# Small filter operations moved from VectorE to GpSimd, a product half split by output block, and a new order in a fused mixer kernel

## The chip, the cores and the metric

The kernel runs on one core of a Trainium2 chip. The metric is device time in microseconds of one execution, as the median of several runs. A core has five engines that run their own queues in order and wait for each other by semaphores: TensorE (PE, matrix products into PSUM), VectorE (DVE), ScalarE (ACT), GpSimd (POOL) and SyncE (SP, which here only issues DMAs). DMAs are also issued from the queues of ScalarE and GpSimd.

## The reference

The inputs are in bfloat16, with S = 2048 positions, D = 640 channels and F = 1536. Two branches of the same input are mixed by a gate of one value a position:

```python
x = A_q
g = sigmoid((x * gate_w).sum(-1, keepdims=True))
# A: a shift convolution of four taps on k, times v, then a causal convolution over the whole length
kv = sum(shifted(k, t) * shift_k[:, ks - 1 - t] for t in range(4)) * v
y  = irfft(rfft(pad(kv)) * rfft(pad(ssm_k)))[:S] + kv * ssm_D      # per channel, length 2S
a  = q * y
# B: an MLP mixer, whose channel quarters are shifted by +1, -1, +2, -2 positions
h  = gelu(layernorm(x) @ w1)
x1 = x + shifted_quarters(h) @ w2
b  = x1 + gelu(layernorm(x1) @ w3) @ w4
out = g * a + (1 - g) * b
```

## The kernel before

**How it is written.** The program first records some 1170 operations, each with its engine, its inputs and its outputs, and derives from the overlaps of their memory which must wait for which. A table `SEQUENCE` then gives the order in which all operations are emitted; each engine gets its own in that order, and runs them in that order. A table `PLACES` gives each PSUM tile its bank, and a tile that takes over a bank waits for the users of the one before. A string `ON` of zeros and ones turns single choices round: each call of `turn(default)` takes the next digit and decides between two engines for one operation (or between an engine and a DMA queue). Nothing is scheduled while the kernel runs.

**The filter.** The long convolution works on chunks of 128 channels (`c` from 0 to 4). `h_load` brings the filter of a chunk, 128 x 2048, and sees it as four blocks of 512 positions. `h_fold` (line 763) adds and subtracts mirrored halves of each block, so that real transforms of half the size do: two large operations (128x1016) on VectorE and, beside them, three small ones, the addition of `ssm_D` to the first column (128x1) and the column in the middle of each block, sum and difference (128x4 each). A copy of column 0 (128x8) reads what the first small one wrote. A transposing DMA then brings positions onto partitions. `h_even` (line 775) splits the even part once more with two large operations (128x1024), and repairs the one row that stands for two positions: a sum and a difference on one partition with 512 elements (1x512), and a copy. `h_chunk` multiplies by the transform matrices on TensorE, and ScalarE copies the result from PSUM.

**The signal.** `kv` computes the four taps and the product with v, `kv2`, `x_fwd` and `combine` transform it likewise. `unit(c)` (line 1017) is the product of the two spectra, block by block: output block o is the sum of filter block a times signal block o - a over a up to o, with three real products for each complex one. It is computed in two halves, output blocks 2 and 3 first, then 0 and 1, with the sums in `ACC` and overwriting the signal's spectrum. `final` does the inverse transform of one output block and one quarter of a block's positions, for channel chunks 0 to 2 (group 0) or 3 and 4 (group 1): four matmuls twice on TensorE, a ScalarE copy, a sum and a difference on VectorE, a matmul that mirrors the difference (`flip`), a ScalarE copy scaled by the gate, and a multiplication with q. Group 0 is added to the output by an accumulating DMA of GpSimd's queue. Group 1 adds branch B's result on VectorE and is stored from SyncE's queue.

**Branch B.** `ln1`, `mm1`, `mm2`, `ln2`, `mm3` and `mm4` are the layer norms and products, on tiles of 128 positions (`t` from 0 to 15). The power -1/2 of each variance is taken on GpSimd (line 869). In `mm1`, the last part of the product holds 32 channels of each quarter and is copied to its shifted places on 32 partitions (line 946): by VectorE, or by a DMA where `turn` says so. `base` scales a tile by 1 - g on ScalarE before it is stored.

Lines that the change and the prediction name: 660 (`tt`, every operation on two tensors), 665 (`ts`), 670 (`act`), 692 (`mm`), 869, 946, and 237 (DMAs).

Of the kernel before, what the change touches and what calls it, by code (L numbers as in the profile page):

```python
# [9 lines left out]
ALU = mybir.AluOpType  # L10
# [436 lines left out]
def bass_gated_mix__ssm_conv_h3__mixer_s_mlp__prompt_kernel(  # L447
# [34 lines left out]
    def ps(n, cls):  # L482
# [3 lines left out]
    SEQUENCE = [1, 4, 5, 6, 26, 7, 3, 45, 24, 8, 0, 49, 50, 51, 55, 48, 68, 9, 10, 11, 12, 13, 14, 15, 16, 69, 17,  # L486
# [66 lines left out]
    ON = ("0000000011111111011011111111111100010000010000101111000000000000001000010010000100000100000100000000"  # L553
          "0000000000000000000000000000000")

    HW = S + 4
    oXF = alloc(20480)
# [611 lines left out]
```

## Time and profile before

| what | value |
|---|---|
| runs | 221.81, 221.84 and 223.04 us; median 221.84 us |
| the profiled execution: its time | 222.27 us |
| its span, first to last instruction | 220.2 us |
| TensorE busy | 209.0 us (95%) |
| VectorE busy, operations | 212.1 us (96%), 418 |
| ScalarE busy | 196.5 us (89%) |
| GpSimd busy | 45.7 us (21%) |
| chain that ended last | VectorE 57%, TensorE 28% |

The profile is of one execution. "Busy" is the time in which at least one instruction of an engine was running. Instructions of one engine overlap a little, so that the mean duration of a group times its count is more than the group's busy time. Rows of groups read: line, engine, operation, output and input with partitions x elements, count, then busy us and mean ns of one, then the idle time before them and what ended it. Rows of the timeline read: start and length in us, engine, line, operation; "x6" there is six instructions merged in one row. The time of an execution holds some 2 us that are outside the span.

### The profile page before, as it was taken

To read this page: it belongs to the slowest core of one execution; us is meant where nothing else is said; L and a number is where in the kernel's file an instruction comes from. 1 tells how busy PE (TensorE), PEld (TensorE's weight loads), DVE (VectorE), ACT (ScalarE), POOL (GpSimd) and SP (SyncE) were. 2 spreads that over 40 slices of the span, in tenths; PEclk is the share of its full clock that TensorE was granted. 3 is DMA by queue.
4 is the path that set the end of the run, shared out by engine and by line. 5 is a ranking of instruction groups with operands and counts; after the bars stand their busy time and mean duration, and the time that the engine had idled before them with its cause. 6 is when DMAs were issued, how large, how long until landed. Compare 5 with 4: busy or idle time off the path is not lost.

```text
span 220.2 us, 3837 instructions
## 1 busy us (share of the span) xinstructions
PE 209.0 (95%) x1401; PEld 125.7 (57%) x1410; DVE 212.1 (96%) x418; ACT 196.5 (89%) x326; POOL 45.7 (21%) x48
## 2 busy tenths in 40 slices
PE   6899999999999999999999999999999999999961
PEld 2598755554664446665446565456665445776730
DVE  5999999999999999999999999999999998999993
ACT  2499999999999999999999999999798978558981
POOL 1331102400010001001380103331101060645440
PEclk9999999999999999999999999999999999999995
DMA  6999998999979995898486893793198299366696
GB/s 170 346 233 214 246 207 231 177 236 193 284 246 204 383 198 95 162 174 185 120 147 110 201 193 43 163 174 71 19 160 182 65 219 246 39 74 71 74 179 119
DMA packets 79440, 37.73 MB, mean 171 GB/s; under 512 B 59001, under 2 KB 76990, under 8 KB 79422
## 3 DMA queue, kind: packets, MB, share of 16 engines
q1 hardware_dynamic: 73920, 31.91, 63.3%
q0 software_dynamic: 5328, 5.51, 18.9%
q8 instruction: 11, 0.18, 0.3%
q10 hardware_dynamic: 174, 0.07, 0.2%
q14 instruction: 7, 0.06, 0.1%
HBM read 14.88 MB, written 5.77 MB: 94 GB/s over the span
## 4 chain that ended last, share of the span: by engine, by line
DVE 57%; PE 28%; DMA 5%; ACT 5%; issue 3%; SPq 0%
DVE arena L660 46%; PE PSall L692 28%; ACT arena L670 5%; DVE arena L665 4%; DMA arena<-arena 3%; DVE arena L861 3%; DVE arena L980 2%; DMA arena<-in_A_q_dram 2%; DVE arena L946 1%; DVE arena L862 0%; DVE arena L866 0%; SPq L237 0%; DVE arena L735 0%; DVE arena L704 0%
## 5 line engine op out<-in xcount | busy, mean ns | idle before, releaser
L692 PE MATMUL PSall<-arena 128*128 128x512 bf16 (+5 forms) x1340 | 201.7, 309 | 3.4 <-ACT arena L670 1.3
L660 DVE TENSOR_TENSOR arena<-arena 128x1024 bf16<-128x1024 bf16 (+14 forms) x270 | 175.1, 712 | 1.7 <-DMA arena<-arena 0.9
L692 PEld LDWEIGHTS PSall<-arena 128*128 128x128 bf16 x1349 | 121.6, 98 | 82.7 <-ACT arena L670 3.3
L670 ACT ACTIVATE arena<-PSall 128x512 bf16<-128x512 f32 (+7 forms) x157 | 94.1, 659 | 9.6 <-PE PSall L750 4.9
L670 ACT ACTIVATE arena<-arena 128x640 bf16<-128x640 bf16 (+5 forms) x107 | 93.5, 904 | 1.9 <-DVE arena L660 1.8
L237 POOL DMA_DIRECT2D out_dram<-arena x24 | 24.1, 1133 | 67.7 <-ACT arena L670 51.7
L869 POOL TENSOR_TENSOR arena<-arena 128x2 f32<-128x2 f32 (+2 forms) x15 | 17.3, 1157 | 58.0 <-DVE arena L866 42.3
L670 ACT ACTIVATE arena<-PSall,arena 128x640 bf16<-128x640 f32 (+2 forms) x32 | 20.5, 652 | 6.8 <-PE PSall L692 6.6
L237 POOL DMA_DIRECT2D arena<-arena x5 | 4.9, 978 | 43.2 <-DVE arena L660 43.2
L980 DVE SCALAR_TENSOR_TENSOR arena<-PSall,arena 128x640 bf16<-128x640 f32 x16 | 12.9, 816 | 0.3
L665 DVE TENSOR_SCALAR arena<-arena 128x640 bf16<-128x640 bf16 (+6 forms) x35 | 11.9, 358 | 0.1
L861 DVE BATCH_NORM_STATS2 arena<-arena 128x6 f32<-128x320 bf16 x20 | 9.0, 484 | 1.3 <-DMA arena<-in_A_q_dram 1.3
L715 PE MATMUL PSall<-arena 128*128 128x512 bf16 x15 | 5.4, 529 | 2.2 <-DVE arena L712 2.2
L670 ACT ACTIVATION_READ_ACCUMULATOR arena<-arena 128x1 f32 x28 | 5.7, 204 | 0.0
L946 DVE TENSOR_SCALAR arena<-arena 32x256 bf16<-32x256 bf16 (+1 forms) x22 | 5.3, 240 | 0.4
L715 PEld LDWEIGHTS PSall<-arena 128*128 128x128 bf16 x15 | 1.8, 128 | 5.0 <-issue 2.5
L922 PE MATMUL PSall<-arena 128*128 128x128 bf16 x40 | 3.4, 220 | 0.9 <-DVE arena L665 0.9
L922 PEld LDWEIGHTS PSall<-arena 128*128 128x128 bf16 x40 | 2.4, 97 | 1.3 <-DVE arena L665 1.3
L866 DVE SCALAR_TENSOR_TENSOR arena<-arena 128x2 f32<-128x2 f32 (+2 forms) x19 | 2.9, 155 | 0.0
L718 ACT ACT_TABLE_LOAD x1 | 1.3, 1283 | 1.3 <-PEq L1154 1.3
L862 DVE BATCH_NORM_AGGREGATE arena<-arena 128x2 f32<-128x12 f32 x10 | 1.7, 192 | 0.0
L980 DVE DVE_READ_ACCUMULATOR arena<-PSall,arena 128x1 f32 x16 | 1.3, 80 | 0.0
(19 smaller groups left out, 2.9 us busy)
## 6 DMA issues: line engine op xcount, KB each, us to landing
arena<-in_A_ssm_k_dram SPq DMA_DIRECT2D x5, 512.0 KB, 5.2
arena<-in_A_q_dram SPq DMA_DIRECT2D x6, 320.0 KB, 5.7
arena<-in_B_w_dram SPq DMA_DIRECT2D x1, 1920.0 KB, 8.4
out_dram<-arena SPq DMA_DIRECT2D x16, 96.0 KB, 3.9
arena<-arena POOLq DMA_DIRECT2D x4, 384.0 KB, 5.0
out_dram<-arena POOLq DMA_DIRECT2D x16, 96.0 KB, 3.6
arena<-in_A_q_dram SPq DMA_DIRECT2D x8, 192.0 KB, 4.1
out_dram<-arena POOLq DMA_DIRECT2D x8, 192.0 KB, 4.0
```

Of the source, the lines that this page charges most:

```text
L237: fn = lambda e: e.dma_start(out, in_, **kw)
L660: P.op(eng, lambda e: e.tensor_tensor(o, real(a), real(b), op), [a, b], [o], dve_ns(o, [a, b], 2) if eng == "dve" else 500)
L665: P.op(eng, lambda e: e.tensor_scalar(o, real(a), s1, s2, op0=op0, **({} if op1 is None else {"op1": op1})), [a] + aps, [o], dve_ns(o, [a] ...
L670: P.op("act", lambda e: e.activation(real(o), real(a), f, bias=bias, scale=scale, **({"accum_out": accum} if accum is not None else {})), ...
L692: fns.append(lambda e, l=l, r=r, i=i: e.matmul(real(o), l, r, start=(i == 0), stop=(i == last)))
L715: P.op("pe", lambda e: e.matmul(real(pw), warm[:, 0:128], warm[:, 128:640], start=True, stop=True), [warm], [pw], 427.0 if i < 14 else 216.0)
L861: P.op("dve", lambda e, o=o, i=i: e.bn_stats(o, i), [i], [o], 400)
L866: P.op("dve", lambda e: e.scalar_tensor_tensor(o, a, x, b, op0=op0, op1=op1), [a, b] + aps, [o], n_of(o) / 0.96 + 65)
L869: P.op("pool", lambda g: g.tensor_tensor(o, a, e, ALU.pow), [a, e], [o], dur)
L922: P.op("pe", [lambda e, c=c, pb=pb, xn=xn: e.transpose(real(pb)[:, 128 * c:128 * (c + 1)], xn[:, 128 * c:128 * (c + 1)], ident) for c in r ...
L946: P.op("dve", lambda e, o=hT[q, 4, c0:c0 + n], i=hx[q, :]: e.tensor_scalar(o, i, 1.0, None, op0=ALU.mult), [hx[q, :]], [hT[q, 4, c0:c0 + n ...
L980: P.op("dve", lambda e: e.scalar_tensor_tensor(x, real(pr), 1.0, x, op0=ALU.mult, op1=ALU.add, accum_out=st[1, 0][:, t:t + 1]), [pr, x], [ ...
```

## The change

Seven things change; the sums and products that are computed stay the same.

1. In `h_fold`, three small operations a chunk (128x1, 128x4, 128x4), and in `h_even` two (1x512 each), go from VectorE to GpSimd: 25 operations in all. `ON` has zeros for all of them.
2. For the fifth chunk (`c == 4`), the second half of `unit` is computed as output block 1 and then output block 0, each with its own products, sum and copy, where both were computed together. This has five operations more, of half the size; the added copy is on VectorE by `ON`.
3. Two of the copies of `mm1` that were DMAs of SyncE's queue are VectorE's, by `ON`.
4. The copies of `mm1` on VectorE have one more read, the column ahead of the one they write first, which orders them behind the copy that writes there.
5. The scaling of tile 6 in `base` goes from ScalarE to VectorE, by `ON`.
6. `SEQUENCE` is new: the order of all operations.
7. `PLACES` is new: the PSUM banks of all tiles.

```diff
-    SEQUENCE = [1, 4, 5, 6, 26, 7, 3, 45, 24, 8, 0, 49, 50, 51, 55, 48, 68, 9, 10, 11, 12, 13, 14, 15, 16, 69, 17,
...
+    SEQUENCE = [7, 1, 6, 4, 8, 27, 5, 25, 2, 26, 0, 28, 45, 48, 46, 50, 49, 51, 53, 55, 69, 9, 10, 11, 68, 52, 12,
...
+    def small_tt(o, a, b, op):
+        tt(o, a, b, op, "dve" if turn(False) else "pool")
...
     def h_fold(c):
 
         k, fo = kst[c], kfo[c]
-        tt(k[:, 0, 0:1], k[:, 0, 0:1], Dcol[:, c:c + 1], ALU.add)
+        small_tt(k[:, 0, 0:1], k[:, 0, 0:1], Dcol[:, c:c + 1], ALU.add)
...
-            tt(fo[:, e, :, 128], k[:, :, 384], k[:, :, 128], op)
+            small_tt(fo[:, e, :, 128], k[:, :, 384], k[:, :, 128], op)
...
-        tt(o[0:1, 0, 0], ev[0:1, 1, :, 0], ev[0:1, 0, :, 0], ALU.add)
-        tt(o[0:1, 1, 0], ev[0:1, 1, :, 0], ev[0:1, 0, :, 0], ALU.subtract)
+        small_tt(o[0:1, 0, 0], ev[0:1, 1, :, 0], ev[0:1, 0, :, 0], ALU.add)
+        small_tt(o[0:1, 1, 0], ev[0:1, 1, :, 0], ev[0:1, 0, :, 0], ALU.subtract)
...
-                         [hx[q, :]], [hT[q, 4, c0:c0 + n]], n / 3.84 + 65)
+                         [hx[q, :], hT[q, 4, c0 - 1:c0]], [hT[q, 4, c0:c0 + n]], n / 3.84 + 65)
...
-        for o0 in (2, 0):
-            for a in range(o0 + 2):
+        for o0, o1 in ((2, 4), (0, 2)) if c < 4 else ((2, 4), (1, 2), (0, 1)):
+            for a in range(o1):
                 lo = max(o0, a)
-                n, x0 = o0 + 2 - lo, lo - a
-                acc, tmp = ACC[:, lo - o0:2], TT[:, 0:n]
+                n, x0 = o1 - lo, lo - a
+                acc, tmp = ACC[:, lo - o0:o1 - o0], TT[:, 0:n]
...
-            Y = XF[:, c, o0:o0 + 2]
-            tt(Y[:, :, 0], ACC[:, :, 2], ACC[:, :, 1], ALU.subtract)
-            tt(Y[:, :, 1], ACC[:, :, 2], ACC[:, :, 0], ALU.add)
-            scale(Y[0:1, :, :, 0:128], ACC[0:1, :, 0:2, 0:128], 1.0, True)
+            Y, R = XF[:, c, o0:o1], ACC[:, 0:o1 - o0]
+            tt(Y[:, :, 0], R[:, :, 2], R[:, :, 1], ALU.subtract)
+            tt(Y[:, :, 1], R[:, :, 2], R[:, :, 0], ALU.add)
+            scale(Y[0:1, :, :, 0:128], R[0:1, :, 0:2, 0:128], 1.0, True)
```

Three places show how the order moves. The first is GpSimd's queue from its first operation on, before: the powers of the layer norms, and then the accumulating DMAs of products (128x1536) and of output tiles.

```order
L869 TENSOR_TENSOR arena<-arena 128x1 x4
L869 TENSOR_TENSOR arena<-arena 128x2 x6
L869 TENSOR_TENSOR arena<-arena 128x4 x2
L237 DMA arena<-arena 128x1536
L237 DMA out_dram<-arena 128x384 x2
L237 DMA arena<-arena 128x2x1536
```

The same queue from the same place now, where line 872 is the power and line 660 the small operations of the filter.

```order
L872 TENSOR_TENSOR arena<-arena 128x1 x4
L872 TENSOR_TENSOR arena<-arena 128x2 x2
L660 TENSOR_TENSOR arena<-arena 128x4
L660 TENSOR_TENSOR arena<-arena 128x1
L660 TENSOR_TENSOR arena<-arena 128x4
L872 TENSOR_TENSOR arena<-arena 128x2 x2
L660 TENSOR_TENSOR arena<-arena 128x4
L660 TENSOR_TENSOR arena<-arena 1x512
L660 TENSOR_TENSOR arena<-arena 128x1
L660 TENSOR_TENSOR arena<-arena 128x4
L660 TENSOR_TENSOR arena<-arena 1x512
L872 TENSOR_TENSOR arena<-arena 128x2 x2
```

The filter's operations stand between the powers, and further on between the DMAs too.

The second place is the head of VectorE's queue behind the constants, before. BN_STATS and BN_AGGR are the statistics of half a tile and of a tile, the 128x1 TENSOR_SCALAR is the step from a tile's variance to GpSimd's power, and the 128x640 one the normalised tile.

```order
L861 BN_STATS arena<-arena 128x6 x2
L862 BN_AGGR arena<-arena 128x2
L665 TENSOR_SCALAR arena<-arena 128x1
L861 BN_STATS arena<-arena 128x6 x3
L862 BN_AGGR arena<-arena 128x2
L704 MEMSET arena 128x5
L665 TENSOR_SCALAR arena<-arena 128x1
L861 BN_STATS arena<-arena 128x6
L665 TENSOR_SCALAR arena<-arena 128x640
```

And the same place now.

```order
L864 BN_STATS arena<-arena 128x6 x2
L865 BN_AGGR arena<-arena 128x2
L864 BN_STATS arena<-arena 128x6
L665 TENSOR_SCALAR arena<-arena 128x1
L864 BN_STATS arena<-arena 128x6 x3
L865 BN_AGGR arena<-arena 128x2 x2
L665 TENSOR_SCALAR arena<-arena 128x1
L665 TENSOR_SCALAR arena<-arena 128x640
```

A statistic of another tile (tile 1) now stands ahead of the first tile's variance step.

The third place is VectorE's queue at the end of the fifth product unit, before: 128x2x1024, 128x2x512, 128x1536 and the like are the unit's, 128x768 is a multiplication of a `final`.

```order
L660 TENSOR_TENSOR arena<-arena 128x1024
L660 TENSOR_TENSOR arena<-arena 128x2x512
L660 TENSOR_TENSOR arena<-arena 128x512
L660 TENSOR_TENSOR arena<-arena 128x2x1024
L660 TENSOR_TENSOR arena<-arena 128x768
L660 TENSOR_TENSOR arena<-arena 128x1536
L660 TENSOR_TENSOR arena<-arena 128x2x512 x2
```

And now, where 128x256 and 128x384 are sums and differences of a `final` of group 1 and group 0.

```order
L660 TENSOR_TENSOR arena<-arena 128x1024 x2
L660 TENSOR_TENSOR arena<-arena 128x512
L660 TENSOR_TENSOR arena<-arena 128x384
L660 TENSOR_TENSOR arena<-arena 128x1536
L660 TENSOR_TENSOR arena<-arena 128x256 x2
L660 TENSOR_TENSOR arena<-arena 128x512 x2
L660 TENSOR_TENSOR arena<-arena 128x768
L660 TENSOR_TENSOR arena<-arena 128x512
L660 TENSOR_TENSOR arena<-arena 128x768
L660 TENSOR_TENSOR arena<-arena 128x1024
```

Output block 1 is finished (128x512 x2) before the products of output block 0 (128x512 and 128x1024), and work of `final` stands between them.

More of the change, by code (lines that the diff above doesn't have):

```diff
@@ L484, in ps @@
         return v if n == 1 else v.rearrange("p (b n) -> p b n", b=2)
-    SEQUENCE = [1, 4, 5, 6, 26, 7, 3, 45, 24, 8, 0, 49, 50, 51, 55, 48, 68, 9, 10, 11, 12, 13, 14, 15, 16, 69, 17,
[59 rows of a table removed]
-    PLACES = [4, 1, 7, 6, 5, 4, 6, 1, 1, 7, 0, 6, 3, 0, 2, 1, 3, 2, 3, 6, 7, 2, 1, 2, 7, 3, 5, 0, 3, 6, 4, 1, 1, 6,
[6 rows of a table removed]
-    ON = ("0000000011111111011011111111111100010000010000101111000000000000001000010010000100000100000100000000"
-          "0000000000000000000000000000000")
+    SEQUENCE = [7, 1, 6, 4, 8, 27, 5, 25, 2, 26, 0, 28, 45, 48, 46, 50, 49, 51, 53, 55, 69, 9, 10, 11, 68, 52, 12,
[59 rows of a table added]
+    PLACES = [2, 1, 1, 1, 4, 1, 6, 3, 0, 2, 4, 2, 5, 2, 7, 7, 4, 3, 7, 3, 1, 6, 3, 6, 1, 2, 5, 0, 5, 4, 3, 0, 2, 1,
[6 rows of a table added]
+    ON = ("0000000011111111111111111111000001111000000001000000000010000000001011110000000000000010000100100000"
+          "000010000010000010000000100000010000000000000000000000000")
     HW = S + 4
```

130 rows, old and new, of tables (PLACES, SEQUENCE) are left out of this document.

## The prediction

> **What bounds the kernel now.** I read the busy times first, then a table of stretches, because a share over the whole span mixes head, body and tail. In the table the columns are stretch and length, then busy us (and instructions) of TensorE, its weight loads, VectorE, ScalarE and GpSimd, then the granted clock and the DMA.
>
> ```profile
> PE 209.0 (95%) x1401; PEld 125.7 (57%) x1410; DVE 212.1 (96%) x418; ACT 196.5 (89%) x326; POOL 45.7 (21%) x48
> ...
> DVE 57%; PE 28%; DMA 5%; ACT 5%; issue 3%; SPq 0%
> ...
> 0.00:2.16 2.16, 0.00 (x1) 0.01 (x1) 1.02 (x8) 0.81 (x1) 0.20 (x4) 1.00 0.15 34
> 2.16:14.62 12.46, 11.43 (x117) 7.51 (x117) 11.10 (x42) 6.40 (x21) 3.17 (x5) 1.00 1.07 289
> 14.62:199.40 184.78, 183.92 (x1189) 108.81 (x1195) 182.57 (x318) 174.41 (x277) 35.40 (x33) 1.00 0.83 172
> 199.40:211.60 12.20, 11.92 (x94) 8.95 (x94) 12.13 (x35) 11.82 (x24) 5.69 (x5) 1.00 0.74 87
> 211.60:215.50 3.90, 1.70 (x7) 0.41 (x5) 3.87 (x15) 2.47 (x6) 1.19 (x1) 0.83 0.79 179
> 215.50:220.20 4.70, 0.00 (x0) 0.00 (x0) 1.38 (x5) 0.59 (x2) 0.00 (x0) 0.50 0.67 125
> ```
>
> TensorE and VectorE are both full. TensorE's idle time, row by row, is 2.16 + 1.03 + 0.86 + 0.28 + 2.20 + 4.70 = 11.23 us; in the 185 us of the body it is 0.86. The change leaves every matmul in place. So taking work from VectorE can shorten the run only by shrinking one of these six pieces, and the body's is nearly nothing. That is the main reading: at 96% VectorE looks like the limit, but beside it stands an engine with 0.86 us to give.
>
> **VectorE's work.** Prices are means of groups by shape.
>
> ```profile
> L660 DVE TENSOR_TENSOR arena<-arena 128x1024 bf16<-128x1024 bf16 x80 | 52.0, 682 | 1.0 <-DMA arena<-arena 0.9
> L660 DVE TENSOR_TENSOR arena<-arena 128x2048 bf16<-128x2048 bf16 x40 | 48.1, 1214 | 0.1
> L660 DVE TENSOR_TENSOR arena<-arena 128x1536 bf16<-128x1536 bf16 x16 | 15.1, 947 | 0.2 <-ACT arena L670 0.2
> L670 ACT ACTIVATE arena<-arena 128x384 bf16<-128x384 bf16 x24 | 14.4, 608 | 0.0
> L660 DVE TENSOR_TENSOR arena<-arena 128x512 bf16<-128x512 bf16 x22 | 9.0, 417 | 0.1
> L665 DVE TENSOR_SCALAR arena<-arena 128x640 bf16<-128x640 bf16 x16 | 6.6, 430 | 0.0
> L660 DVE TENSOR_TENSOR arena<-arena 1x512 bf16<-1x512 bf16 x10 | 4.1, 408 | 0.0
> L946 DVE TENSOR_SCALAR arena<-arena 32x256 bf16<-32x256 bf16 x15 | 3.3, 219 | 0.2
> L946 DVE TENSOR_SCALAR arena<-arena 32x512 bf16<-32x512 bf16 x7 | 2.0, 287 | 0.1
> L660 DVE TENSOR_TENSOR arena<-arena 128x4 bf16<-128x4 bf16 x10 | 1.6, 166 | 0.0
> L665 DVE TENSOR_SCALAR arena<-arena 128x8 bf16<-128x8 bf16 x5 | 0.9, 181 | 0.0
> L660 DVE TENSOR_TENSOR arena<-arena 128x1 bf16<-128x1 bf16 x5 | 0.8, 150 | 0.0
> ```
>
> Neighbours on VectorE overlap, so a mean is more than an operation takes from the engine. The row at 141.11 below holds two operations of 1536 and two of 1024 elements: 2 x 0.947 + 2 x 0.682 = 3.26 us of means in 3.02 us, 0.08 per joint.
>
> *Removed* (filter folding and even part, five channel chunks): 10 one-row operations x (0.408 - 0.08) + 10 of four columns x (0.166 - 0.08) + 5 of one column x (0.150 - 0.08) = 3.28 + 0.86 + 0.35 = 4.5 us.
>
> *Added.* Two copies of the first product, which SyncE's DMA queue did: 0.219 + 0.287 = 0.51 us, or 0.35 with the joints off; I take 0.5. The read added to all these copies, one column of the copy before, can make each wait for its forerunner, which costs it its joint at most: 0 to 24 x 0.08 = 1.9 us. I take 0, since other operations stand between most of them.
>
> One scaling of 384 columns comes from ScalarE (0.608 us there): between 0.181 (8 columns) and 0.430 (640), near the latter, less 0.08: 0.25 us. The split of product unit 5: four operations become two each, one of 2048 elements into 2 x 1024 and three of 1024 into 2 x 512. A pair costs 2 x 0.682 - 0.08 - 1.214 = 0.07 us more, or 2 x 0.417 - 0.08 - 0.682 = 0.07, so 0.3 us for the four, and there is one more one-row copy, 0.1 to 0.33 by the rows 181 and 408: 0.2. Sum 0.5 + 0.25 + 0.3 + 0.2 = 1.3 us. VectorE loses 4.5 - 1.3 = 3.2 us net. ScalarE loses 0.6 us, SyncE two issues; neither ends the run, and I count both as nothing.
>
> **GpSimd's work.** No row shows GpSimd adding. The nearest are its powers, and the timeline around three of them.
>
> ```profile
> L869 POOL TENSOR_TENSOR arena<-arena 128x2 f32<-128x2 f32 x8 | 8.1, 1017 | 29.5 <-DVE arena L866 20.3 <-DVE arena L665 9.2
> L869 POOL TENSOR_TENSOR arena<-arena 128x4 f32<-128x4 f32 x3 | 6.7, 2231 | 22.0 <-DVE arena L866 22.0
> L869 POOL TENSOR_TENSOR arena<-arena 128x1 f32<-128x1 f32 x4 | 2.5, 629 | 6.5 <-DVE arena L665 6.5
> ...
> 35.21 1.22 DVE L660 TENSOR_TENSOR arena<-arena 128x2048 bf16<-128x2048 bf16 x1
> 35.37 1.61 POOL L869 TENSOR_TENSOR arena<-arena 128x2 f32<-128x2 f32 x1 [11.53 <-DVE arena L866]
> 36.46 1.29 DVE L660 TENSOR_TENSOR arena<-arena 128x1024 bf16<-128x1024 bf16 x2
> ...
> 141.11 3.02 DVE L660 TENSOR_TENSOR arena<-arena 128x1536 bf16<-128x1536 bf16 x4
> 141.28 2.21 POOL L869 TENSOR_TENSOR arena<-arena 128x2 f32<-128x2 f32 x2 [5.28 <-DVE arena L866]
> ...
> 109.89 3.99 POOL L869 TENSOR_TENSOR arena<-arena 128x4 f32<-128x4 f32 x1
> ```
>
> GpSimd's power of 35.37 ends at 36.98, 0.55 us after VectorE's operation beside it (36.43); the lone 128x1 takes 0.63. So GpSimd seems to wait until VectorE's running operation is over; another, at 109.89, took 3.99 us. VectorE lost nothing: two operations from 36.46 take 1.29 us = 2 x 0.682 - 0.08, while the power still runs. The Trainium skill, "SBUF — State Buffer", section "SBUF: two separate sides", says that a VectorE operation with two SBUF inputs and a GpSimd operation that reads SBUF shut each other out for a whole instruction, the first to start winning. The trace agrees for GpSimd's waiting and not for VectorE's, with 0.55 us of overlap; but a power reads at most four elements a lane, a one-row operation 512 of each input. The skill's "GPSIMD Engine Reference", section 3.1, puts two-input work at about 2.6 cycles an element: an estimate of 1.1 us for 512 at its 1.2 GHz, 11 us for ten; no run here shows it.
>
> GpSimd's own time grows by 25 x 0.63 to 25 x 2.23 = 16 to 56 us, and it is idle for 174. What counts is who waits. Behind them in GpSimd's queue stand the layer norms' powers and the accumulating DMAs; ahead, VectorE's copy of column 0, the transposing DMA and TensorE's filter matmuls. The new order puts several VectorE operations or other matmuls between most of these results and their use, so I take 0; bound 0 to 25 x 0.63 = 16 us (a wait added brings no gain). VectorE's loss by being held: 0 by the timeline, or one GpSimd duration for each one-row operation.
>
> **The new order.** *Head.*
>
> ```profile
> 4.23 0.15 DVE L665 TENSOR_SCALAR arena<-arena 128x1 f32<-128x1 f32 x1
> ...
> 5.52 0.50 DVE L861 BATCH_NORM_STATS2 arena<-arena 128x6 f32<-128x320 bf16 x1 [0.34 <-DMA arena<-in_A_q_dram]
> ...
> 6.63 0.43 DVE L665 TENSOR_SCALAR arena<-arena 128x640 bf16<-128x640 bf16 x1
> ...
> 7.11 0.45 PE L922 MATMUL PSall<-arena 128*128 128x128 bf16 x5
> ...
> 8.56 0.45 PE L922 MATMUL PSall<-arena 128*128 128x128 bf16 x5 [0.86 <-DVE arena L665]
> ```
>
> A statistic of a tile that lands at 5.5 us now stands ahead of the first tile's variance step. That step ran at 4.2 us and would run near 6; then power 0.6, normalising 0.43: the first transposes go from 7.11 to about 8. The small constant matmuls fill part of this, and the wait of 0.86 at 8.56 shrinks. I take 0, bounds -0.5 to +0.9 us. *Body*: 0.86 us of idle time can go, a new order can add as much: 0, bounds -0.9 to +1.
>
> *Tail.*
>
> ```profile
> 183.78 33.16 DVE L660 TENSOR_TENSOR arena<-arena 128x1024 bf16<-128x1024 bf16 x74 [0.89 <-DMA arena<-arena]
> ...
> 213.31 0.28 PE L692 MATMUL PSall<-arena 128*128 128x256 bf16 x1 [1.16 <-ACT arena L670]
> 214.04 0.29 PE L692 MATMUL PSall<-arena 128*128 128x256 bf16 x1 [0.45 <-DVE arena L660]
> 214.82 0.61 PE L692 MATMUL PSall<-arena 128*128 128x256 bf16 x2 [0.49 <-DVE arena L660]
> ```
>
> VectorE works without a break to the end; TensorE ends with flips that wait 1.16 + 0.45 + 0.49 = 2.1 us. Here the 3.2 us and the split tell: unit 5 is done sooner, and fewer outputs wait at the end. But the last output still goes inverse transform, copy, add and subtract, flip, scale, multiply, store, whichever it is. So at most the 2.1 us go, and at least 0. Three turns between engines remain whatever the order, so I take a quarter, 0.5 us.
>
> **Sum.** 220.2 - 0.5 = 219.7 us of span. The profiled execution took 222.27 us, 0.43 above the runs' median of 221.84; the forecast for the median is 221.84 - 0.5 = **221.3 us**. The bounds of head, body and tail (-0.5 - 0.9 - 2.1, +0.9 + 1) rarely meet, so this case alone gives 219.8 to 223.0.
>
> **Rivals.** Within 1% of the median (2.2 us) is what a measurement of this kernel cannot tell from no change.
>
> *No change* (forecast): chance 0.49.
>
> *VectorE is held by GpSimd's one-row operations.* Ten times one GpSimd duration, by the 128x2 row 1.02 us, 10.2 us on VectorE; the 3.2 us saved pay first, 7 us remain: about 229 us. By 0.63 and 2.23 us it is +3 and +19. It shows once each costs over 0.32 us, and passes 1% from about 0.55. This is the skill's lock, above, taken the other way round. For it: ten times 512 elements against four, and GpSimd's waits. Against: not one VectorE operation is lengthened in the rows. Chance 0.34.
>
> *Late results.* If a GpSimd result takes 3.99 us as at 109.89, users with little between wait; two such stalls of 2 us on TensorE, with no slack there, give +4: 226 us. Chance 0.05.
>
> *VectorE is the limit after all* (the chain of waits, quoted second at the top, is VectorE's for 57%): the whole 3.2 us come through, 218.6 us. Against it stand the 0.86 us. Chance 0.12.
>
> **Range and chances.** Low end 219.4 leaves out most of the last rival (0.08), high end 229.0 about half of the lock's upper part (0.12). Faster 0.12, same 0.49, slower 0.34 + 0.05 = 0.39.
>
> **What would show it.** Right: VectorE busy near 209, TensorE's busy time unchanged and its idle in the body still under 2 us, one-row group on GpSimd, VectorE's 1024 and 2048 means at 682 and 1214. Lock: those means or VectorE's idle time grow beside GpSimd's one-row operations, and TensorE idles by several us in the body. Late results: TensorE or SyncE waits on GpSimd by name. Wrong on the other side: VectorE's end moves by 3 us with TensorE's idle in the tail gone.

## The result and the profile after

The changed kernel takes 232.41 us as a median (232.11 to 232.84, 4 runs) against 221.82 us before: a ratio of 1.0466, 95% interval 1.0424 to 1.0507. It is slower by 10.6 us. The forecast was 221.3 us with a range up to 229.0.

The page of the changed kernel: busy times, five rows of the span in 40 slices (5.8 us each), and the engines' shares of the chain that ended last.

```profile
PE 212.0 (92%) x1400; PEld 125.8 (55%) x1410; DVE 215.3 (93%) x401; ACT 196.2 (85%) x325; POOL 98.5 (43%) x73
...
PE   6999999999899999990899999999999799999980
...
DVE  5999999999999999992949999999999999999994
ACT  2599998999899999809889999999899489956882
POOL 1525271222603049992090099264932233244541
PEclk9999999999999999999599999999999999999998
...
DVE 73%; POOL 13%; ACT 4%; PE 3%; issue 3%; DMA 1%; SPq 0%
```

VectorE was to lose 3.2 us of work and has 3.2 us more (215.3 against 212.1). The span is 230.4 us, so VectorE stands still for 15.1 us, against 8.1 before; TensorE for 18.4 against 11.2. Nearly all of the new idle time is one hole near the middle (the 0 of TensorE's row), and in the slice behind it TensorE's clock is at half. Before, there was no such hole. GpSimd's rows are full just ahead of it, and it now has 13% of the chain.

Groups by shape of the changed kernel show what GpSimd's new work takes, and which VectorE groups grew.

```profile
L660 DVE TENSOR_TENSOR arena<-arena 128x2048 bf16<-128x2048 bf16 x39 | 48.0, 1242 | 4.7 <-ACT arena L670 4.7
L660 POOL TENSOR_TENSOR arena<-arena 1x512 bf16<-1x512 bf16 x10 | 26.4, 2641 | 10.6 <-DVE arena L660 10.6
L660 POOL TENSOR_TENSOR arena<-arena 128x1 bf16<-128x1 bf16 x5 | 15.3, 3058 | 0.0
L660 POOL TENSOR_TENSOR arena<-arena 128x4 bf16<-128x4 bf16 x10 | 14.5, 1464 | 4.3 <-DMA arena<-in_A_ssm_k_dram 4.3
...
L665 DVE TENSOR_SCALAR arena<-arena 128x8 bf16<-128x8 bf16 x5 | 1.9, 378 | 0.1
L869 DVE SCALAR_TENSOR_TENSOR arena<-arena 128x16 f32<-128x16 f32 x1 | 1.1, 1116 | 0.0
L869 DVE SCALAR_TENSOR_TENSOR arena<-arena 128x2 f32<-128x2 f32 x9 | 3.2, 365 | 0.0
L660 DVE TENSOR_TENSOR arena<-arena 128x1016 bf16<-128x1016 bf16 x10 | 6.7, 684 | 0.0
```

The means of GpSimd are odd: one column takes longer than a row of 512 elements. So they are not the work of these operations but mostly waiting. On VectorE the mean of 128x2048 went from 1214 to 1242 ns, that of the short 128x8 copy from 181 to 378 ns, and that of the 128x2 step of the layer norms from 152 to 365 ns.

The timeline of the changed kernel ahead of the hole and in it (start, length, engine, line; GpSimd's rows first):

```profile
84.58 3.08 POOL L660 TENSOR_TENSOR arena<-arena 128x1 bf16<-128x1 bf16 x1
87.62 7.45 POOL L660 TENSOR_TENSOR arena<-arena 1x512 bf16<-1x512 bf16 x1
95.05 8.55 POOL L660 TENSOR_TENSOR arena<-arena 128x4 bf16<-128x4 bf16 x1
103.69 1.14 POOL L660 TENSOR_TENSOR arena<-arena 1x512 bf16<-1x512 bf16 x1
...
87.75 6.30 DVE L660 TENSOR_TENSOR arena<-arena 128x1536 bf16<-128x1536 bf16 x9
93.97 1.15 DVE L665 TENSOR_SCALAR arena<-arena 128x8 bf16<-128x8 bf16 x1
95.89 7.63 DVE L660 TENSOR_TENSOR arena<-arena 128x1024 bf16<-128x1024 bf16 x9
...
103.78 5.04 ACT L670 ACTIVATE arena<-arena 128x2048 bf16<-128x2048 bf16 x4 [6.55 <-POOL arena L660]
108.22 4.88 DVE L660 TENSOR_TENSOR arena<-arena 128x2048 bf16<-128x2048 bf16 x4 [4.71 <-ACT arena L670]
109.53 0.59 PE L695 MATMUL PSall<-arena 128*128 128x512 bf16 x1 [5.68 <-ACT arena L670]
```

Read it from below. TensorE waits 5.68 us for ScalarE, which does not empty PSUM, because a tap of `kv` (128x2048) stands at the head of ScalarE's queue and waits 6.55 us for GpSimd: it writes memory that `h_fold` of the fourth chunk has still to read on GpSimd. That operation, of four columns, starts at 95.05 and ends at 103.6, when VectorE has run out of work; its sibling of the same size follows at once and ends at 103.75. While the first of the two waits, VectorE does nine operations of two inputs without a break. The one-row operation ahead of it waits in the same way for 6.3 us, beside nine more, and gets through when VectorE reaches a copy of one input at 93.97; that copy then takes 1.15 us instead of 0.18. With VectorE still, at 103.69, a one-row operation takes 1.14 us. VectorE then waits for ScalarE twice, 4.7 us up to 108.22 and 3.3 us up to 120.00.

So two things are seen at once: GpSimd is late, and VectorE operations are lengthened beside it. What each is worth, and whether the new order has a part in it, the experiments had to tell.

### The profile page after: what moved, and what is told of

Same layout as the page of the kernel before. It is cut to its first block, busy times and chain, and to the rows that moved or that the text cites. A ratio compares the mean times of both kernels' runs of the same rounds, so it can differ in the third digit from the quotient of the medians.

```text
span 230.4 us, 3850 instructions
## 1 busy us (share of the span) xinstructions
PE 212.0 (92%) x1400; PEld 125.8 (55%) x1410; DVE 215.3 (93%) x401; ACT 196.2 (85%) x325; POOL 98.5 (43%) x73
## 4 chain that ended last, share of the span: by engine, by line
DVE 73%; POOL 13%; ACT 4%; PE 3%; issue 3%; DMA 1%; SPq 0%
DVE arena L660 57%; POOL arena L660 13%; DVE arena L983 5%; DVE arena L665 4%; ACT arena L670 4%; DVE arena L864 3%; PE PSall L695 3%; DVE arena L949 2%; DVE arena L869 2%; DMA arena<-in_A_q_dram 1%; POOL arena L237 1%; DVE arena L865 0%; SPq L237 0%; DVE arena L708 0%
## 5 line engine op out<-in xcount | busy, mean ns | idle before, releaser
L695 PE MATMUL PSall<-arena 128*128 128x512 bf16 (+5 forms) x1339 | 204.6, 312 | 11.3 <-ACT arena L670 6.4
L660 DVE TENSOR_TENSOR arena<-arena 128x1024 bf16<-128x1024 bf16 (+11 forms) x249 | 173.6, 759 | 8.8 <-ACT arena L670 8.0
L670 ACT ACTIVATE arena<-PSall 128x512 bf16<-128x512 f32 (+8 forms) x157 | 94.5, 659 | 14.7 <-PE PSall L695 10.3
L670 ACT ACTIVATE arena<-arena 128x640 bf16<-128x640 bf16 (+6 forms) x106 | 92.2, 901 | 9.0 <-POOL arena L660 6.6
L660 POOL TENSOR_TENSOR arena<-arena 128x4 bf16<-128x4 bf16 (+2 forms) x25 | 55.7, 2253 | 14.9 <-DVE arena L660 10.6
L237 POOL DMA_DIRECT2D out_dram<-arena x24 | 25.2, 1216 | 28.4 <-ACT arena L670 18.5
L872 POOL TENSOR_TENSOR arena<-arena 128x2 f32<-128x2 f32 (+2 forms) x15 | 16.4, 1095 | 38.8 <-DVE arena L869 25.2
L665 DVE TENSOR_SCALAR arena<-arena 128x640 bf16<-128x640 bf16 (+8 forms) x37 | 13.7, 387 | 0.3
L718 PE MATMUL PSall<-arena 128*128 128x512 bf16 x15 | 6.0, 543 | 2.0 <-DVE arena L715 2.0
L869 DVE SCALAR_TENSOR_TENSOR arena<-arena 128x2 f32<-128x2 f32 (+2 forms) x19 | 5.6, 303 | 0.0
```

The costliest lines, as they stand in the source:

```text
L237: fn = lambda e: e.dma_start(out, in_, **kw)
L660: P.op(eng, lambda e: e.tensor_tensor(o, real(a), real(b), op), [a, b], [o], dve_ns(o, [a, b], 2) if eng == "dve" else 500)
L665: P.op(eng, lambda e: e.tensor_scalar(o, real(a), s1, s2, op0=op0, **({} if op1 is None else {"op1": op1})), [a] + aps, [o], dve_ns(o, [a] ...
L670: P.op("act", lambda e: e.activation(real(o), real(a), f, bias=bias, scale=scale, **({"accum_out": accum} if accum is not None else {})), ...
L695: fns.append(lambda e, l=l, r=r, i=i: e.matmul(real(o), l, r, start=(i == 0), stop=(i == last)))
L718: P.op("pe", lambda e: e.matmul(real(pw), warm[:, 0:128], warm[:, 128:640], start=True, stop=True), [warm], [pw], 427.0 if i < 14 else 216.0)
```

## The experiments

Each ratio is to the kernel before, run in turn with it on the same chip. The experiments ran on four chips, on which the kernel before took 221.75 to 222.26 us, so that times of different experiments compare to about half a microsecond. Two theories run through them: "late" (a GpSimd result arrives late, and its user stops) and "held" (a VectorE operation is lengthened beside a GpSimd one).

**One to four: operations back on VectorE, the order untouched.** The first puts all 25 small operations back on VectorE.

```diff
-        tt(o, a, b, op, "dve" if turn(False) else "pool")
+        tt(o, a, b, op, "dve" if turn(False) or True else "pool")
```

> All 25 small operations of the filter are VectorE's again, at the same places of the new order; the split, the copies and the order stay. Theory "late": the loss comes from GpSimd results that arrive late, because an operation of GpSimd finds no opening in VectorE's stream (8.5 us at 95.0 us of the changed kernel's profile), so ScalarE and TensorE stop once, at 103 us; here nothing waits for GpSimd, and the time is that of the kernel before, 219 to 223 us. Theory "held": the loss is VectorE time, ten one-row operations that each lengthen a VectorE operation beside them by about 0.9 us; here too 219 to 223, with VectorE busy near 213. Theory "order": the new order or the split costs it; here the time stays near 232.

Measured: 240.86 us, ratio 1.0842 (1.0795 to 1.0888). No theory of mine allowed for that. The waits of this kernel (who waited for whom: us in total, times, longest):

```profile
DVE arena L660 <- DMA arena<-arena: 10.9, 3, 5.8
...
PE PSall L695 <- DVE arena L660: 8.4, 5, 3.7
...
DVE arena L660 <- DMA arena<-in_A_ssm_k_dram: 4.5, 1, 4.5
```

The order is written for GpSimd. A small operation stands in it where a separate queue can wait for a load, or where that queue would come to it late. On VectorE at the same place it stops the whole stream for the load (4.5 us), or comes so late that TensorE and a transposing DMA wait. The trial changed two things instead of one.

The second keeps the fifteen few-column operations on GpSimd, with `n_of(o) == 512` for `True`.

> The ten one-row operations (1x512) are VectorE's, the fifteen of few columns stay on GpSimd. Theory "held": nothing is left that holds VectorE for long, so 220 to 223 us, and VectorE 128x2048 and 128x2047 means back at 1.21 to 1.22 us. Theory "late": a few-column operation takes 0.2 us when it gets in but can still wait as long as VectorE's stream has no opening, 8.5 and 10.5 us in the changed kernel; but with no one-row operation ahead of it in the queue the one at 95.0 us would pass at the opening of 87.6 us, so 220 to 225, with some few-column operations still over 3 us.

Measured: 234.76 us, ratio 1.0569 (1.053 to 1.0609), far above both ranges. The third does the reverse, with `n_of(o) < 512`.

> The fifteen few-column operations are VectorE's, the ten one-row operations stay on GpSimd. Theory "held": nearly the whole loss stays, 228 to 232 us, with VectorE operations lengthened by 0.9 us beside each of the ten. Theory "late": the operation that stopped ScalarE at 97 to 104 us (128x4 of the fourth chunk's fold) is on VectorE now, so that pause goes; but the second one-row operation of the third chunk can itself wait until VectorE runs dry, and TensorE's filter product behind it; 222 to 231, and where a pause of TensorE remains, GpSimd's one-row operation stands in front of it by name.

Measured: 238.36 us, ratio 1.0767 (1.0695 to 1.0838), above both ranges again. The fourth moves the five around the hole, with `len(P.ops) in (400, 401, 445, 447, 449)`.

> Only the five operations that GpSimd ran between 84.6 and 104.8 us in the changed kernel's profile (two one-row operations of the third chunk, three few-column operations of the fourth) are VectorE's; twenty stay on GpSimd, eight one-row ones among them. Theory "late": the pause at 97 to 110 us and the slower TensorE clock behind it are the loss (TensorE idle 7.2 us more and busy 3.0 us more than before), so 221 to 225 us. Theory "held": eight of ten holds remain, so at most a fifth of the loss goes: 229 to 232 us.

Measured: 232.27 us, ratio 1.0463 (1.0429 to 1.0498), just beyond the upper end of "held". But its timeline has a hole at the same place, from another cause:

```profile
107.66 17.64 PE L695 MATMUL PSall<-arena 128*128 128x512 bf16 x70 [3.36 <-DVE arena L660]
...
115.42 8.39 DVE L660 TENSOR_TENSOR arena<-arena 128x1024 bf16<-128x1024 bf16 x9 [5.47 <-DMA arena<-arena]
```

The second one-row operation of the third chunk, now behind a dozen others on VectorE, holds up TensorE and a transposing DMA as GpSimd had. All four trials suffer from places made for another engine, and their times settle nothing between "late" and "held". VectorE's busy time in them does tell something of "held": it is 215.0 us with all 25 on VectorE, 213.4 with only the few-column operations on GpSimd, and 219.3 with only the one-row operations there, although VectorE then has ten operations fewer to do. So it is the one-row operations that hold it. The trials also show that this order cannot be had without GpSimd, or GpSimd taken out of it, by a switch.

**Five: all on VectorE, each behind its large sibling.**

```diff
+        tt(o, a, b, op, "dve" if turn(False) or True else "pool")
...
+    for i, j in [(285, 284), (283, 286), (287, 286), (339, 338), (337, 338), (341, 340), (393, 392), (391, 394), (395, 394),
+                 (447, 446), (445, 446), (449, 448), (685, 684), (683, 684), (687, 686), (292, 290), (293, 291), (346, 344),
+                 (347, 345), (400, 398), (401, 399), (454, 452), (455, 453), (692, 690), (693, 691)]:
+        SEQUENCE.remove(i)
+        SEQUENCE.insert(SEQUENCE.index(j) + 1, i)
```

> All 25 small operations are VectorE's as in the first run, but each one is moved in the order to right behind the large VectorE operation of the same step with the same inputs (1x512 behind its 128x1024, 128x4 and 128x1 behind their 128x1016), so that none of them waits on VectorE for a load that is still out or stands late. Theory "places": the 241 us of the first run came from places in the order that suit a separate queue and stop VectorE (it waited 4.5 us for a filter load at 45.7 us, and a 1x512 stood behind a dozen others at 107 us); then 219 to 224 us here, and GpSimd's late results are the changed kernel's whole loss. Theory "order": the new order costs VectorE and TensorE time of its own; then 228 or more also here.

Measured: 224.99 us, ratio 1.0144 (1.0111 to 1.0177); the holes are gone.

```profile
PE 210.0 (94%) x1400; PEld 124.8 (56%) x1410; DVE 214.7 (96%) x426; ACT 196.8 (88%) x325; POOL 45.9 (21%) x48
```

That is "places", just beyond its upper end. The 240.86 us were an artefact of the places, and 7.4 of the 10.6 us belong to the work being on GpSimd. But 3.1 us are left, and VectorE has 2.6 us more to do than before (214.7 against 212.1), with 8.4 us idle in a span of 223.1, as against 8.1.

**Six: the old order, and the 25 operations on GpSimd.**

```diff
-        tt(o[0:1, 0, 0], ev[0:1, 1, :, 0], ev[0:1, 0, :, 0], ALU.add)
+        tt(o[0:1, 0, 0], ev[0:1, 1, :, 0], ev[0:1, 0, :, 0], ALU.add, "pool")
...
```

> The kernel before, with its order, banks, copies and undivided unit, and only the 25 small operations put on GpSimd at their places in the old order. Theory "late": GpSimd's operations wait for openings in VectorE's stream here too, so TensorE or ScalarE stop for one of them: 225 to 235 us, with GpSimd operations of over 5 us. Theory "order": the loss belongs to the new order, and the old one gives 219 to 223 us.

Measured: 228.78 us, ratio 1.0301 (1.0275 to 1.0327). The move alone, without the new order, costs 6.9 us. That is the range of "late", and GpSimd operations of over 5 us are there; but by the account below most of it is VectorE's longer busy time. Groups and a row of the timeline:

```profile
L660 POOL TENSOR_TENSOR arena<-arena 1x512 bf16<-1x512 bf16 x10 | 24.0, 2404 | 31.6 <-DVE arena L660 31.6
...
131.18 7.69 POOL L660 TENSOR_TENSOR arena<-arena 128x4 bf16<-128x4 bf16 x1
```

**Seven: openings in VectorE's stream.** Ten copies of one column, which nobody needs, stand between VectorE operations of two inputs.

```diff
+    doors = [375, 399, 389, 413, 647, 737, 442, 738, 761, 702]
+    for j in doors:
+        SEQUENCE.insert(SEQUENCE.index(j) + 1, len(P.ops))
+        P.op("dve", lambda e: e.tensor_scalar(bfs[:, 204:205], ones[:, 0:1], 1.0, None, op0=ALU.mult), [ones[:, 0:1]], [bfs[:, 204:205]], 70)
```

> The changed kernel with ten VectorE operations more: a copy of one column (128x1, one input, to a place nobody reads) between two of the two-input operations, five between 85 and 90 us, three between 133 and 136 us, two near 161 us, where GpSimd's operations took 7 to 10.5 us. Theory "late by starvation": GpSimd gets in beside an operation of one input; its operations of 7.4, 8.5, 10.5 and 7.0 us become 1 to 2.5 us, the pause of 97 to 110 us goes, and the time is 221 to 225 us. Theory "held": each opening lengthens VectorE by up to 1 us, so no gain: 231 to 236 us. If GpSimd's long operations stay long, one-input operations are not what lets it in.

Measured: 228.37 us, ratio 1.0287 (1.0259 to 1.0314): 4.0 us faster than the changed kernel, with more work. Its timeline where the changed kernel had 3.08, 7.45 and 8.55 us, and its busy times:

```profile
85.22 1.28 POOL L660 TENSOR_TENSOR arena<-arena 128x1 bf16<-128x1 bf16 x1
86.46 1.66 POOL L660 TENSOR_TENSOR arena<-arena 1x512 bf16<-1x512 bf16 x1
88.09 0.66 POOL L660 TENSOR_TENSOR arena<-arena 128x4 bf16<-128x4 bf16 x1
...
87.03 0.14 DVE L1144 TENSOR_SCALAR arena<-arena 128x1 bf16<-128x1 bf16 x1
87.09 1.58 DVE L660 TENSOR_TENSOR arena<-arena 128x1016 bf16<-128x1016 bf16 x1
...
PE 210.4 (93%) x1400; PEld 124.3 (55%) x1410; DVE 218.1 (96%) x411; ACT 196.2 (87%) x325; POOL 73.7 (33%) x73
```

GpSimd gets in beside the copies at 86.37 and 87.03, no engine is seen to wait long for it, and VectorE's idle time falls from 15.1 to 8.5 us (226.6 - 218.1). In exchange VectorE's busy time rises from 215.3 to 218.1: the operation behind the copy at 87.03 takes 1.58 us, where its shape took 684 ns as a mean in the changed kernel (last row of its groups above). Neither theory had the size alone: on balance the openings bring 4.0 us, less lateness against more holding.

**Eight and nine: the small work left out.** In both kernels the 25 operations are not done on any engine.

```diff
-        tt(o, a, b, op, "dve" if turn(False) else "pool")
+        turn(False), P.op("dve", None, [], [], 0)
...
+    SEQUENCE = [i for i in SEQUENCE if P.ops[i].fns != [None]]
```

> The changed kernel without the 25 small operations of the filter: no engine does them (the filter's first column, middle columns and repaired rows are left wrong; the middle columns are zeroed once at the start). What remains is the new order, the split and the copies, with nothing of the work that was moved, on VectorE or on GpSimd. Between 225.0 us (all 25 on VectorE behind their large operations) and this lies what VectorE's relief of some 4.5 us is worth. Theory "VectorE is the limit": 220 to 222 us. Theory "TensorE is the limit" (my forecast's reading of 0.86 us idle in the body): 224 to 225 us.

> The kernel before without the 25 small operations, left out in the same way. Theory "VectorE is the limit": 221.9 less most of 4.5 us, so 217.5 to 219.5 us. Theory "TensorE is the limit": 221 to 222 us.

Measured: new order 220.75 us, ratio 0.9941 (0.9919 to 0.9963); old order 221.24 us, ratio 0.9979 (0.9955 to 1.0003). The busy times of the one and of the other:

```profile
PE 208.7 (96%) x1400; PEld 125.8 (58%) x1410; DVE 209.9 (96%) x406; ACT 196.1 (90%) x325; POOL 45.5 (21%) x48
```

```profile
PE 208.7 (95%) x1401; PEld 125.9 (57%) x1410; DVE 208.7 (95%) x398; ACT 195.8 (89%) x326; POOL 45.3 (21%) x48
```

The old order came out as "TensorE is the limit" had it, the new one as "VectorE is the limit" had it. In the old order the whole of this work, done on VectorE, is worth 0.8 us: VectorE loses 3.4 us and the span only 1.2 (220.2 to 219.0), with VectorE's idle time up from 8.1 to 10.3. In the new order the same work is worth 4.2 us (224.99 to 220.75): VectorE loses 4.8 us and the span 4.7 (223.1 to 218.4), and TensorE's idle time between 14.6 and 199 us falls from 4.1 to 1.3. So there VectorE sets the time once the small work is on it. That this is because VectorE has 1.2 us more to do in the new order is my reading; the fifth run also has its own places for the 25.

**Ten: GpSimd additions whose results nobody uses.** The kernel before, and ten one-row additions of a constant on GpSimd beside it.

```diff
+        x, y = ones[0:1].unsqueeze(1).to_broadcast([1, 4, 128]), AR[0:1, oR + 1536:oR + 2048].rearrange("p (b n) -> p b n", b=4)
+        tt(y, x, x, ALU.add, "pool")
```

> The kernel before, with its 25 small operations on VectorE as they were, and ten GpSimd additions of 1x512 more, one behind each one-row operation in the order, that read a constant and write to a place nobody reads: only what ten such operations do to VectorE, and to GpSimd's own queue, with no result that anyone waits for. Theory "held": VectorE's operations beside them are lengthened by 0.7 to 0.9 us each, 7 to 9 us in all, and the time is 226 to 230 us, with VectorE busy over 218 us. Theory "late only": nobody waits, so 222 to 223 us.

Measured: 226.77 us, ratio 1.0218 (1.0199 to 1.0237).

```profile
PE 209.2 (93%) x1401; PEld 124.9 (56%) x1410; DVE 218.2 (97%) x418; ACT 197.5 (88%) x326; POOL 63.9 (28%) x58
...
L660 POOL TENSOR_TENSOR arena<-arena 1x512 bf16<-1x512 bf16 x10 | 20.1, 2014 | 0.3
```

This is "held" by itself, a little less than the 7 to 9 us worked out. VectorE does the same 418 operations and is busy 6.1 us longer, and the time grows by 4.8 us. No other change was made, and nobody waits for a result of these ten.

**Eleven and twelve: the few-column operations alone.** Eleven is the kernel of the ten copies, with the one-row operations on VectorE behind their siblings.

> The kernel with the ten one-column VectorE copies (228.4 us) once more, but with the ten one-row operations on VectorE, each right behind its large operation; only the fifteen few-column operations are on GpSimd. Theory "the one-row operations alone hold VectorE": its 8.0 us of lengthened operations go and ten times 0.33 us come, so VectorE busy 213 to 214 us and the time 223 to 224.5 us. If few-column operations hold it too, or come late in spite of the copies: 226 us or more.

Measured: 224.87 us, ratio 1.0141 (1.0112 to 1.0169), 0.4 us above what I had worked out; VectorE is busy 214.5 us. The 3.5 us that went are the one-row operations' holding, less what they cost on VectorE. But one few-column operation came late in spite of the copies, with nobody waiting for it:

```profile
86.32 8.29 POOL L660 TENSOR_TENSOR arena<-arena 128x4 bf16<-128x4 bf16 x1
...
88.92 0.14 DVE L1144 TENSOR_SCALAR arena<-arena 128x1 bf16<-128x1 bf16 x1
```

Four of the ten copies ran while it waited, the one of the row above and those at 86.55, 89.58 and 90.24. So a copy in the stream is no sure opening. Twelve is the kernel before with only the fifteen few-column operations on GpSimd.

```diff
-        tt(k[:, 0, 0:1], k[:, 0, 0:1], Dcol[:, c:c + 1], ALU.add)
+        tt(k[:, 0, 0:1], k[:, 0, 0:1], Dcol[:, c:c + 1], ALU.add, "pool")
...
-            tt(fo[:, e, :, 128], k[:, :, 384], k[:, :, 128], op)
+            tt(fo[:, e, :, 128], k[:, :, 384], k[:, :, 128], op, "pool")
```

> The kernel before, with only its fifteen few-column operations on GpSimd. If they neither hold VectorE nor come late, VectorE is busy 1.2 us less and TensorE sets the time: 221 to 222 us, the only part of the move that could come free. If one of them waits for an opening where TensorE or ScalarE need it (with all 25 on GpSimd one took 7.7 us at 131 us): 223 to 226 us.

Measured: 220.75 us, ratio 0.9957 (0.9935 to 0.9978; 10 runs against 13). Its busy times and two rows of its timeline:

```profile
PE 209.3 (96%) x1410; PEld 126.0 (58%) x1410; DVE 211.1 (96%) x403; ACT 196.1 (90%) x326; POOL 69.4 (32%) x63
...
83.99 8.19 POOL L660 TENSOR_TENSOR arena<-arena 128x4 bf16<-128x4 bf16 x1
125.97 7.69 POOL L660 TENSOR_TENSOR arena<-arena 128x4 bf16<-128x4 bf16 x1
```

This version beats both kernels, by a little: 0.4% under the kernel before, about as much as leaving all the small work out. Two of its operations wait about 8 us here too, but no engine is seen to wait for a result of GpSimd, and VectorE's operations are not lengthened.

**The account.** The spans put together, each from the page of its profile:

| kernel | span | VectorE busy | VectorE idle | TensorE idle |
|---|---|---|---|---|
| before | 220.2 | 212.1 | 8.1 | 11.2 |
| before, 25 left out | 219.0 | 208.7 | 10.3 | 10.3 |
| before, few-column 15 on GpSimd | 219.0 | 211.1 | 7.9 | 9.7 |
| before, 25 on GpSimd | 227.0 | 215.3 | 11.7 | 17.1 |
| before, ten unused additions on GpSimd | 224.6 | 218.2 | 6.4 | 15.4 |
| changed, 25 left out | 218.4 | 209.9 | 8.5 | 9.7 |
| changed, 25 on VectorE behind siblings | 223.1 | 214.7 | 8.4 | 13.1 |
| changed, with ten openings | 226.6 | 218.1 | 8.5 | 16.2 |
| changed | 230.4 | 215.3 | 15.1 | 18.4 |

The last row stands 12.0 us above "changed, 25 left out", which has the same order and none of the moved work: 5.4 us are VectorE's longer busy time (held), 6.6 us its idle time (late). With the openings the second part goes to nothing and the first grows to 8.2, the ten copies included. In the old order the same difference is 8.0 us, 6.6 held and 1.4 late: being late in this size belongs to the new order, being held to both.

## Why the prediction was wrong

**What bounds the kernel: right, and read to one side only.** With 0.86 us to give in the body of the kernel before, TensorE lets next to nothing through: leaving out all of the small work there brings 0.8 us, where the forecast gave VectorE's relief 0.5. That did not carry over to the new order, where the same work is worth 4.2 us. But VectorE's row said as much of itself: 8.1 us idle in a span of 220.2. What is added there comes through nearly whole: 4.8 us of time for 6.1 us of lengthened operations. I used the main reading to cap the gain and not to price the risk.

**VectorE's work: close.** Removed 4.5 us: the left-out runs show 3.4 in the old order (212.1 - 208.7) and 4.8 in the new (214.7 - 209.9); why these two differ is open. Added 1.3 us: 209.9 - 208.7 = 1.2.

**The new order: right within the measurement.** Without the small work it is 0.5 us better than the old one (220.75 against 221.24), with intervals that meet. The forecast had -0.5, all of it in the tail, and counted there VectorE's relief too, which these two runs share. Against the kernel before, order and relief together bring 1.25 us (222.00 to 220.75), and not from the tail alone: TensorE's idle time from 2.2 to 14.6 us falls from 1.03 to 0, a term that the forecast put at 0 with a bound of -0.5; from 199 us on it falls from 7.3 to 6.4, and between these it rises from 0.7 to 1.3. The order does no harm of its own; but it was the order in which GpSimd's late results met a waiting ScalarE.

**GpSimd's work: the step that failed, in both of its terms.** "VectorE's loss by being held: 0 by the timeline" measured 5.4 us. The evidence was three rows of powers of two or four elements a lane; they showed that GpSimd waits for VectorE, and no VectorE operation lengthened. That they read too little to hold anything is my reading now, not a run's. They bound the price of a few-column operation, which indeed is nothing, and say little of 512 elements. By that reading the nearest row in form was not near in what counts, the time for which SBUF is read. A one-row operation that gets in while VectorE works lengthens one VectorE operation by about 0.9 us (the single 128x16 one from 216 ns in the kernel before to 1116); six of the ten did so, and the others ran while VectorE stood still or beside operations that were not lengthened. The first row here is of the kernel before; the others are five lengthened operations of the changed kernel, and the sixth is the copy at 93.97, shown above.

```profile
L866 DVE SCALAR_TENSOR_TENSOR arena<-arena 128x16 f32<-128x16 f32 x1 | 0.2, 216 | 0.0
...
28.92 2.06 DVE L660 TENSOR_TENSOR arena<-arena 128x2047 bf16<-128x2047 bf16 x1
56.91 1.12 DVE L869 SCALAR_TENSOR_TENSOR arena<-arena 128x16 f32<-128x16 f32 x1
58.81 2.17 DVE L660 TENSOR_TENSOR arena<-arena 128x2048 bf16<-128x2048 bf16 x1
165.56 1.12 DVE L869 SCALAR_TENSOR_TENSOR arena<-arena 128x2 f32<-128x2 f32 x1
167.73 1.11 DVE L869 SCALAR_TENSOR_TENSOR arena<-arena 128x2 f32<-128x2 f32 x1
```

Over the usual times of their shapes (1.21 to 1.22 us for the two large ones, 0.15 for 128x2, 0.22 for 128x16, 0.18 for the copy) the six are 5.6 us longer, which makes the 5.4 us.

The Trainium skill, "SBUF — State Buffer", section "SBUF: two separate sides", has the two shut each other out for a whole instruction. Five of the six lengthened operations, of two inputs, agree with it (about 0.9 us longer each); the copy at 93.97 has one input. I set the rule aside for rows that could not test it. The Trainium skill, "GPSIMD Engine Reference", section 3.1, gave an estimate of 1.1 us for a one-row operation; the row at 103.69 shows 1.14.

**"I take 0" for late results: 6.6 us of VectorE's idle time**, inside the bound of 0 to 16. I looked for VectorE operations or matmuls between a result and its use, and found several nearly everywhere. That was a count for an operation that lasts 1 us. It may last 10, because the VectorE operations that fill the distance are the same that keep GpSimd out. And the user that stopped was none of those I named (the copy of column 0, the transposing DMA, the filter's matmuls), but ScalarE's tap, which needs the same memory.

**The rivals: both came, and I had them as alternatives.** "VectorE is held by GpSimd's one-row operations" was priced at 229 and "Late results" at 226, each with its cause alone; "Late results" got 0.05. Their added costs together, 7 and 4 us on 222, make 233 against 232.4 measured, but that is luck: VectorE's busy time rose by 3.2 us and not by 7, its idle time by 7.0 and not by 4. One cause feeds both, as I read it: the same exclusion either stops GpSimd or stops VectorE. The row with 3.99 us for a 128x4 power, quoted in the prediction, was the sign of the first kind and was taken for an exception.

**What would show it** held in the main: the mean of 128x2048 and the idle time of VectorE grew, and TensorE idled by several us in the body. The mean of 128x1024 hardly moved (682 to 685 ns), and the wait by GpSimd's name is ScalarE's, where I had named TensorE and SyncE.

## What to carry to other kernels

When two engines are both full, taking work from one of them can gain almost nothing (0.8 us here for all the small work, in the old order), while what lengthens that engine's operations is paid nearly in full (4.8 us of time for 6.1): price a move by what it can add, and not only by what it takes away. A small operation that goes to GpSimd beside a VectorE stream of two-input operations can take its wait for an opening, and not its duration, so look for who needs its result and its memory within 10 us, on every queue. And a small operation that is moved back needs a place of its own in the order, or the trial measures the place.

## What the runs showed of the hardware

**GpSimd can be passed over many times.** In the changed kernel a 128x1 operation that takes 0.33 us elsewhere took 10.53 us beside twelve VectorE operations of two inputs in a row:

```profile
49.53 0.33 POOL L660 TENSOR_TENSOR arena<-arena 128x1 bf16<-128x1 bf16 x1
...
132.84 10.53 POOL L660 TENSOR_TENSOR arena<-arena 128x1 bf16<-128x1 bf16 x1
...
133.08 10.24 DVE L660 TENSOR_TENSOR arena<-arena 128x2048 bf16<-128x2048 bf16 x12
```

By the profile it had started ahead of all twelve. The Trainium skill, "SBUF — State Buffer", section "SBUF: two separate sides", has the first to start win; here twelve that started later went first, so that rule does not tell who waits in such a stream. After its longest waits GpSimd got in at copies of one input (93.97, and 87.03 with the openings), beside short f32 operations such as the 128x2 one at 165.56, and when VectorE ran dry. But in the eleventh an operation was passed over at four such copies, and in the seventh one got in between two 128x1016 operations, at 88.09. So what decides it stays open; a copy put there helped in the seventh and is no sure remedy.

**Where a one-row operation has a price, one VectorE operation pays it**: the short one itself (181 ns to 1.15 us at 93.97) or the next (0.68 to 1.58 us behind the copy at 87.03). It need not have two inputs: in the tenth the mean of the 32x512 copies went from 287 to 506 ns. Operations of one or four columns had no such price: with fifteen of them on GpSimd the 128x2048 operations of VectorE keep their mean:

```profile
L660 DVE TENSOR_TENSOR arena<-arena 128x2048 bf16<-128x2048 bf16 x40 | 48.1, 1213 | 0.3 <-ACT arena L670 0.3
```

**TensorE's clock is lower behind a pause.** In the stretch with the hole, the columns being busy times of TensorE, its weight loads, VectorE, ScalarE and GpSimd, and then the granted clock:

```profile
90.00:103.80 13.80, 13.66 (x88) 8.41 (x87) 13.52 (x17) 7.09 (x14) 13.80 (x4) 1.00 0.42 103
103.80:120.00 16.20, 10.04 (x35) 3.99 (x36) 8.43 (x10) 14.20 (x17) 5.59 (x6) 0.79 0.73 142
```

The clock is 0.79 there and 1.00 ahead of it, and TensorE's busy time over the whole span is 3.3 us longer than in the same order without the moved work (212.0 against 208.7), for the same matmuls. ScalarE, for which VectorE waits 3.3 us up to 120.00, had itself waited for matmuls there. How much of the loss is the clock's, no run here separates.
